# Zeroing the lists and the output from a small resident tile, spread over the steps of the attention, in a fused attention, MLP and top-2 MoE kernel

## The chip, the cores and the metric

One Trainium2 chip, of which the kernel uses a single core. Times are device microseconds of one execution. A core has a matrix engine (PE), whose weight loads show separately as PEld, a vector engine (DVE), an activation engine (ACT), a general engine (POOL) and a queue processor that does nothing but issue transfers (SP). Each runs its own list of instructions in order; they meet only through semaphores. Transfers that SP issues go through one hardware queue (q1) on the core's 16 DMA engines, transfers that POOL issues through a software queue (q0) on the same 16.

## The reference

```python
def _attn_ref(q, k, v, n_sink, window):           # 2 batches, 8 heads, 768 tokens, head size 64
    scores = scale * np.matmul(q, k.transpose(0, 1, 3, 2))
    keep = is_sink | in_window                    # 4 sink tokens, window of 128
    a = softmax(np.where(keep, scores, -1e9))
    return np.matmul(a, v)
def _moe_ref(x, w_in, w_out):                     # 1536 tokens, 512 -> 2048 -> 512
    h = x @ w_in
    return (h - np.tanh(h)) @ w_out
def _moe2_ref(x, w_gate, w_noise, noise, w1, w2): # 8 experts, 512 -> 1024 -> 512
    noisy_logits = x @ w_gate + np.log1p(np.exp(x @ w_noise)) * noise
    top2 = the two largest of each token; top2_w = softmax over these two
    out = np.zeros((N, D))
    for e, k: out[mask] += top2_w * (relu(x[mask] @ w1[e]) @ w2[e])
```

The three run one after the other on the same 1536 tokens.

## The kernel before

**Attention.** The tokens lie in 12 blocks of 128 (6 of each batch). A block has four pairs of heads, and a pair goes through PE (scores), DVE (L382: scale, mask and minimum), ACT (L395: exponential), POOL (L406: normalization), PE (L453: transposes) and PE again (L486: product with v). Each block needs its q, its k and its v, 256 KB each, loaded by SP (`att_load`, L260). Blocks 0 to 5 load k and v in place; from block 6 on a load lands in one of four `qr` buffers, ACT casts it (L289 q, L301 k, L314 v) and POOL takes the remainder (L290, L302, L315), which frees the buffer for a load some places later. In the listings `qr8_1` is the load of block 8's k (0 is q, 1 k, 2 v).

**First MLP.** From block 2 on its first layer (L606) and second layer (L638) run between the pairs. Its 96 steps `n` (a chunk of 256 tokens, a 128-wide piece of the hidden layer) are written out in order in the main loop; the first 24 run during the attention. Each piece of weights (`rawi`, `rawo`, 1 MB) is loaded by SP and split into two words by ACT and DVE (`split_d`, L202, with L215 on ACT and L216 on DVE as the first readers of a load). Two raw buffers of each kind are in turn, so a load waits for the split of the one two before it.

**Lists and output.** The router sends each token's row to two of 9 lists in device memory, `xs`, each a section of 1664 rows of 520 floats. The rows that an expert may read are zeroed ahead (`clear_rows`, L865): nine sections, for each one transfer of the rows in use (L871: 384, 512 or 256 rows, up to 1040 KB) and one of the last 8 floats of the rows that are left (L874: 36 to 44 KB in runs of 32 bytes). They read a zero tile that shares buffers (`x2T`) with the router. `route_setup` (L660) zeroes the whole output, 3 MB, by one transfer on POOL's queue (L675), and loads the router's small tables `wg_sb` (L661) and `noise_sb` (L662); DVE splits `wg_sb` into `wg_r` (L663, L664).

**Order.** The program is written in one sequence; a scheduler puts each engine's instructions in order from dependences and the written sequence, and may move an instruction far ahead of where it is written if it is ready. SP has eight semaphores in turn for its transfers: a transfer also waits for the one eight before it to have landed.

```python
        if n == 22:
            route_setup()
        if n == 56:
            clear_rows()
```

Of the kernel before, what the change touches and what calls it, by code (L numbers as in the profile page):

```python
# [9 lines left out]
F32 = mybir.dt.float32  # L10
# [6 lines left out]
P = 128  # L17
# [54 lines left out]
def kernel(ctx: ExitStack, tc: tile.TileContext, qkv, vsink, w64, wm, wgn, noise, out,  # L72
                                  n_sink, window):
    nc = tc.nc
    PSUM = bass.MemoryType.PSUM
    NBLK = qkv.shape[0]
    S = 768
    NB = S // P
    NT = NBLK * P
    E = 8  # L80
# [32 lines left out]
    cst = ctx.enter_context(tc.tile_pool(name="cst", bufs=1))  # L113
# [5 lines left out]
    PITCH = 520  # L119
# [472 lines left out]
    def a_at(n):  # L592
        g, c, u = seq[n]
        return g, c, u, 2 * g + u // 2

    def a_l1(n):
        g, c, u, d = a_at(n)
        w = wsp["i", d]
        s = u % 2
        h = bank("h", f"h{n}")  # L600
        hp[n] = h
        x, ts = x_cols(c * CT, (c + 1) * CT)
        t = 0
        for wa, xa in ((0, 0), (0, 1), (1, 0)):
            for k in range(4):
                nc.tensor.matmul(h[:, :CT], w[:, wa, k * 256 + s * P:k * 256 + (s + 1) * P],  # L606
                                 x[:, k, xa, ts], start=t == 0, stop=t == 11)
                t += 1

    def a_chain(n):  # L610

        h = hp.pop(n)
        th = gp.tile([P, CT], F32, tag="th", name=f"th{n}", bufs=2)
        nc.scalar.activation(th, h[:, :CT], AF.Tanh)  # L614
        yield
        nc.vector.tensor_sub(th, h[:, :CT], th)  # L616
        yield
        g = gp.tile([P, 2, CT], F32R, tag="g", name=f"g{n}", bufs=3)
        nc.scalar.copy(g[:, 0], th)  # L619
        yield  # L620
        nc.vector.tensor_sub(g[:, 1], th, g[:, 0].bitcast(F32))  # L621
        gt[n] = g
        yield

    def a_l2(n):
        gi, c, u, d = a_at(n)
        g = gt.pop(n)
        w = wsp["o", d]
        s = (u % 2) * 512
        end = c >= LATE  # L630
        first = u == 0 and not (end and gi == 3)
        done = u == 3 and not (end and gi == 2)
        if first:
            turn.reverse()
            acc[c] = [bank(turn[0] if gi else "a", f"acc{n}_{m}") for m in range(CB)]
        for m in range(CB):
            for t, (ga, wa) in enumerate(((0, 0), (1, 0), (0, 1))):
                i = nc.tensor.matmul(acc[c][m], g[:, ga, m * P:(m + 1) * P], w[:, wa, s:s + 512],  # L638
                                     start=first and t == 0, stop=done and t == 2)
        last_mm[0] = i  # L640
        if done:
            if gi == 0:
                x2s[c] = gp.tile([P, CB, PITCH], F32, tag="x2", name=f"x2_{c}", bufs=NC)
            for m in range(CB):
                x = x2s[c][:, m, :512]
                if gi == 0:
                    nc.scalar.copy(x, acc[c][m])
                else:
                    nc.vector.tensor_add(x, acc[c][m], x)
# [10 lines left out]
    def route_setup():  # L660
        nc.sync.dma_start(wg_sb, wgn)  # L661
        nc.sync.dma_start(noise_sb, noise)  # L662
        nc.vector.tensor_copy(wg_r[:, :, 0], wg_sb)  # L663
        nc.vector.tensor_sub(wg_r[:, :, 1], wg_sb, wg_r[:, :, 0].bitcast(F32))  # L664
        nc.gpsimd.memset(ones, 1.0)
        nc.gpsimd.memset(tri, 1.0)

        nc.gpsimd.affine_select(out=tri, in_=tri, compare_op=ALU.is_gt, fill=0.0, base=0,
                                pattern=[[1, P]], channel_multiplier=-1)
        nc.gpsimd.iota(idx, pattern=[[1, E]], base=0, channel_multiplier=0,  # L670
                       allow_small_or_imprecise_dtypes=True)
        nc.gpsimd.memset(macc, 0.0)
        zero = gp2.tile([P, 512], F32, tag="x2T", name="zero", bufs=2)
        nc.gpsimd.memset(zero, 0.0)
        nc.gpsimd.dma_start(out.rearrange("(t p) d -> p t d", p=P), zero[:, None, :].to_broadcast([P, NBLK, 512]))  # L675

    scat = []
    pend = []
# [179 lines left out]
    def width(v):  # L858
        return WA if v == 0 else WB if v == E else W
# [2 lines left out]
        w = width(v)  # L862
        return [(m, o, min(P, w - o)) for m, o in enumerate(range(0, w, P))]

    def clear_rows():  # L865

        zero = gp2.tile([P, 512], F32, tag="x2T", name="zrow", bufs=2)
        nc.gpsimd.memset(zero, 0.0)
        for v in range(E + 1):
            n = (width(v) + P - 1) // P  # L870
            nc.sync.dma_start(xs[v * SEC:v * SEC + n * P].rearrange("(p m) (b d) -> p (m b) d", p=P, b=2),  # L871
                              zero[:, None, :PITCH // 2].to_broadcast([P, 2 * n, PITCH // 2]))
            o = v * SEC + n * P
            nc.sync.dma_start(xs[o:(v + 1) * SEC, 512:].rearrange("(p m) d -> p m d", p=P),  # L874
                              zero[:, None, :8].to_broadcast([P, SEC // P - n, 8]))
        for c in range(NC):
            nc.gpsimd.memset(x2s[c][:, :, 518:], 0.0)
            for o in (0, 1):
                nc.gpsimd.iota(x2s[c].bitcast(I32)[:, :, 512 + o:513 + o], pattern=[[P, CB], [0, 1]],
                               base=c * CT + o * FAR, channel_multiplier=1)  # L880
# [251 lines left out]
    def mark():  # L1132
        return len(nc.cur_bb.bb.instructions)
# [22 lines left out]
    def emit(k, last):  # L1156

        while k > 0:
            if cur[0] is None:
                if not todo_split or todo_split[-1][1] > last:  # L1160
                    return
                cur[0] = todo_split.pop()
                cur.append(split_d(*cur[0]))
            try:
                next(cur[1])
                k -= 1
            except StopIteration:
                if cur[0][1] < 8 or cur[0][0] == "o" and cur[0][1] != EARLY_D:
                    load_next()
                cur[:] = [None]  # L1170

    def need(kind, d):
        while (kind, d) not in wsp:
            emit(1, d)
# [4 lines left out]
    def attend(k):  # L1179
        for _ in range(k):  # L1180
            next(slots, None)
            ns[0] += 1

    def attend_chunk(c):

        if not wide:
            attend(2 * (4 * CB * (c + 1) + LEND) - ns[0])
# [36 lines left out]
    def pull_routes():  # L1224
        if routes:
            with tc.high_priority():
                try:
                    next(routes[0])
                except StopIteration:
                    routes.pop(0)  # L1230

    gp2 = None
# [3 lines left out]
    for n in range(-3, N1):  # L1236
        marks["a", n] = mark()
        g, c, u, d = a_at(max(n, 0))
        ch = a_chain(n + 2) if 0 <= n + 2 < N1 else iter(())
        if n + 3 < N1:  # L1240
            g2, c2, u2, d2 = a_at(n + 3)
            if g2 == 0 and u2 == 0:
                attend_chunk(c2)
                if c2 == NC - 1:
                    if not wide:
                        att_ctx.__exit__(None, None, None)
                    gp2 = ctx.enter_context(tc.tile_pool(name="gp2", bufs=2))
                    ring[1] = gp2
            need("i", d2)
        last = min(2 * g + 3, 7) if gp2 else 1  # L1250
        m = g == 0 and n >= 0
        next(ch, None)
        if m:
            attend(1)
        next(ch, None)
        if n + 3 < N1:
            a_l1(n + 3)
        if m:
            attend(1)
        next(ch, None)  # L1260
        if n >= N1 - 7:
            emit((1, 1, 1, 1, 1, 1, 0)[n - N1 + 7], 11)
        elif g < 3 or n % 4 == 1:
            emit(1, last)
        if m:
            attend(1)
        next(ch, None)
        if n >= 0:
            need("o", d)
            a_l2(n)  # L1270
        if m:
            attend(1)
            emit(1, last)
        if n == 22:
            route_setup()
        if n == 56:
            clear_rows()
        if n >= 0 and g == NG1 - 1 and u == 3 and (c % 2 or c >= LATE):
            routes.append(route(c if c >= LATE else c - 1, c + 1))
            ends.append(c + 1)  # L1280
        if n < N1 - 1:
            for _ in range(3 if n <= PAIR else 2):
                pull_routes()
            issue(2 if PAIR <= n < PAIR + 4 else 1)
        if n == PAIR + 4:
            assert len(scat) == 2 * LATE * CB and not pend, (n, len(scat), len(pend))
            b_gather(0)
        if N1 - 3 <= n < N1 - 1:
            b_trans(0, (2 * (n - N1 + 3), 2 * (n - N1 + 3) + 1))
# [17 lines left out]
    for n in range(N1, N):  # L1307
        marks["a", n] = mark()
        e, u, d = b_at(n)
# [120 lines left out]
```

## Time and profile before

| | us |
|---|---|
| three runs, median (lowest to highest) | 774.65 (772.66 to 775.27) |
| profiled execution, its own time | 772.26 |
| span in its trace, first to last instruction | 770.0 |
| PE busy | 723.9 (94%) |
| DVE busy | 475.9 (62%) |
| ACT busy | 356.3 (46%) |
| POOL busy | 186.4 (24%) |
| granted PE clock, mean | 0.979 |

The rows come from one profiled execution, and lie on its clock, which begins with the span. The trace has each engine's instructions with the idle time ahead of them and what ended it. A row of SP is an issue: its duration is the time that SP was held, not the time of the transfer. [...]

### The profile page before, as it was taken

Reading aid. Unit: us, or ns where it says so; the run is one execution under the profiler, and the core shown is the slowest. Engines: PE = TensorE matmul, PEld = TensorE weight load, DVE = VectorE, ACT = ScalarE, POOL = GpSimd, SP = SyncE. Lnnn points to the kernel's source line nnn. Section 1 sums busy time; section 2 is a strip of 40 time slices with the busy share of each in tenths; the row PEclk is TensorE's granted clock in tenths of the full one; section 3 lists DMA queues with packets and bytes.
Section 4 is the critical chain, followed back from the end, with each engine's and each line's share of the span. In section 5 each row is a group of like instructions: output and inputs, shape, how many; then the busy total and the mean of one; then the engine's idle time right before and its main releaser. Section 6 shows DMA issues by size and latency. Waiting matters only on the chain.

```text
span 770.0 us, 12093 instructions
## 1 busy us (share of the span) xinstructions
PE 723.9 (94%) x4346; PEld 653.0 (85%) x4346; DVE 475.9 (62%) x1203; ACT 356.3 (46%) x785; POOL 186.4 (24%) x219
## 2 busy tenths in 40 slices
PE   6878999999699999999999979999999999999991
PEld 3565788888699999988888979999999999899991
DVE  5998678877587587446467766776646474544221
ACT  4977688776353344234346534444343434332110
POOL 4444355531000000000351231313131313132321
PEclk9999899999899999999999999999999999999996
DMA  7453111006998133000225388756757444444421
GB/s 263 138 178 109 56 51 61 2 1 206 297 287 233 56 110 110 1 1 1 84 112 167 125 237 237 213 164 194 193 186 192 164 155 160 143 139 165 143 84 35
DMA packets 62117, 104.96 MB, mean 136 GB/s; under 512 B 19629, under 2 KB 45869, under 8 KB 55392
## 3 DMA queue, kind: packets, MB, share of 16 engines
q1 hardware_dynamic: 54528, 80.20, 34.9%
q0 software_dynamic: 7376, 22.85, 8.7%
q10 hardware_dynamic: 144, 1.05, 0.3%
q8 instruction: 36, 0.59, 0.3%
q14 instruction: 33, 0.27, 0.1%
HBM read 79.12 MB, written 25.68 MB: 136 GB/s over the span
## 4 chain that ended last, share of the span: by engine, by line
PE 44%; issue 24%; DMA 15%; POOL 6%; DVE 6%; ACT 3%; POOLq 0%; SPq 0%; ACTq 0%; DVEq 0%
PE h L606 16%; PE acc L638 15%; DMA prev<-out,tab 6%; DMA out<-y,tab 5%; PE xb L486 4%; POOL out L1030 4%; PE s L371 3%; DMA rawo<-w 2%; POOL prev L883 2%; PE pt L453 2%; DVE e L382 1%; DMA rawi<-wm 1%; ACT e L395 1%; PE x2p L695 1%; PE y L1002 1%
## 5 line engine op out<-in xcount | busy, mean ns | idle before, releaser
L606 PE MATMUL h<-xT,wi 128*128 128x256 f32 x1152 | 160.9, 287 | 7.9 <-DVE th L616 5.9
L606 PEld LDWEIGHTS h<-xT,wi 128*128 128x128 f32 x1152 | 153.1, 192 | 14.9 <-DVE th L616 6.4
L978 PE MATMUL h<-xg,wi 128*128 128x424 f32 (+1 forms) x768 | 157.6, 354 | 4.0 <-ACT xg L961 3.9
L1002 PE MATMUL y<-hh,wo 128*128 128x424 f32 (+1 forms) x768 | 152.0, 347 | 0.7 <-DVE yt L1016 0.5
L638 PE MATMUL acc<-wo,g 128*128 128x512 f32 x576 | 151.1, 396 | 0.0
L978 PEld LDWEIGHTS h<-xg,wi 128*128 128x128 f32 x768 | 138.6, 190 | 8.7 <-ACT xg L961 5.0
L1002 PEld LDWEIGHTS y<-hh,wo 128*128 128x128 f32 x768 | 139.4, 188 | 4.1 <-DVE yt L1016 0.9
L638 PEld LDWEIGHTS acc<-wo,g 128*128 128x128 f32 x576 | 101.9, 189 | 16.5
L988 ACT ACTIVATE hh<-h 128x424 fp32r<-128x424 f32 (+1 forms) x64 | 32.6, 511 | 149.9 <-PE h L978 147.6
L1030 POOL DMA_INDIRECT out<-y,tab x33 | 41.4, 1255 | 189.7 <-DVE y L1029 189.4
L808 POOL DMA_INDIRECT xs<-x,sl x24 | 26.0, 1085 | 235.7 <-DVE th L616 183.7
L989 DVE SCALAR_TENSOR_TENSOR hh<-h,hh 128x424 fp32r<-128x424 f32 (+1 forms) x64 | 37.0, 578 | 73.9 <-ACT hh L988 69.8
L406 POOL TENSOR_TENSOR e<-e,nm 128x528 f32<-128x528 f32 (+1 forms) x48 | 50.1, 1044 | 81.3 <-DVE nm L404 45.5
L616 DVE TENSOR_TENSOR th<-h,th 128x256 f32<-128x256 f32 x96 | 40.4, 420 | 39.6 <-ACT th L614 37.1
L614 ACT ACTIVATE th<-h 128x256 f32<-128x256 f32 x96 | 36.6, 382 | 59.5 <-PE h L606 56.0
L619 ACT CAST g<-th 128x256 fp32r<-128x256 f32 x96 | 38.7, 404 | 55.0 <-PE acc L638 37.7
L395 ACT ACTIVATE e<-e,nm 128x264 f32<-128x264 f32 (+1 forms) x96 | 47.2, 492 | 22.5 <-DVE nm L382 20.3
L621 DVE TENSOR_TENSOR g<-th,g 128x256 fp32r<-128x256 f32 x96 | 43.2, 450 | 22.3 <-ACT g L619 21.4
L486 PE MATMUL xb<-pT,v 128*128 128x256 f32 x220 | 49.1, 352 | 3.6 <-DVE xT L501 2.2
L232 DVE TENSOR_TENSOR wi<-rawi,wi 128x1024 fp32r<-128x1024 f32 x32 | 39.1, 1223 | 21.6 <-ACT wi L231 21.5
L883 POOL DMA_INDIRECT prev<-out,tab x33 | 35.6, 1080 | 44.0 <-DMA out<-y,tab 34.6
L486 PEld LDWEIGHTS xb<-pT,v 128*128 128x128 f32 x220 | 33.7, 197 | 13.5 <-issue 5.3
(172 smaller groups left out, 888.8 us busy)
## 6 DMA issues: line engine op xcount, KB each, us to landing
rawi<-wm SPq DMA_DIRECT2D x31, 1024.0 KB
rawi<-w SPq DMA_DIRECT2D x8, 1024.0 KB
rawo<-w SPq DMA_DIRECT2D x8, 1024.0 KB
xs<-zrow SPq DMA_DIRECT2D x7, 1040.0 KB
xr<-xs SPq DMA_DIRECT2D x28, 224.0 KB
qr<-qkv SPq DMA_DIRECT2D x23, 256.0 KB
rawc<-wm SPq DMA_DIRECT2D x4, 1024.0 KB
out<-zero POOLq DMA_DIRECT2D x1, 3072.0 KB
```

What stands on the lines that cost most here:

```text
L232: nc.vector.tensor_sub(t[:, 1], r, t[:, 0].bitcast(F32))
L395: nc.scalar.activation(e[:, h], e[:, h], AF.Exp, bias=nm[:, h, 0:1], scale=-1.0, accum_out=nm[:, h, 2:3])
L406: nc.gpsimd.tensor_mul(e, e, nm[:, :, 3:4].to_broadcast([P, 2, C]))
L486: nc.tensor.matmul(o, l, r_, start=t == 0, stop=t == len(todo) - 1)
L606: nc.tensor.matmul(h[:, :CT], w[:, wa, k * 256 + s * P:k * 256 + (s + 1) * P], x[:, k, xa, ts], start=t == 0, stop=t == 11)
L616: nc.vector.tensor_sub(th, h[:, :CT], th)
L621: nc.vector.tensor_sub(g[:, 1], th, g[:, 0].bitcast(F32))
L638: i = nc.tensor.matmul(acc[c][m], g[:, ga, m * P:(m + 1) * P], w[:, wa, s:s + 512], start=first and t == 0, stop=done and t == 2)
L883: nc.gpsimd.indirect_dma_start(out=dst, out_offset=None, in_=src[:rows], in_offset=bass.IndirectOffsetOnAxis(ap=t[:n, m, c:c + 1], axis=0) ...
L978: nc.tensor.matmul(h[:, :width(e)], w[:, wa, k * 256 + s * P:k * 256 + (s + 1) * P], xg[e][:, k, xa, :width(e)], start=t == 0, stop=t == 11)
L1002: nc.tensor.matmul(yacc[e][m][:, :width(e)], w[:, wa, s + m * P:s + (m + 1) * P], g[:, ga], start=u == 0 and t == 0, stop=u == NU2 - 1 and ...
L1030: i = nc.gpsimd.indirect_dma_start(out=out[:, :], out_offset=bass.IndirectOffsetOnAxis(ap=t[:n, m, 1:2], axis=0), in_=y, in_offset=None, b ...
```

## The change

The zero tile becomes 128x260 and lives in the pool of constants. The nine sections go out one per step from step 2 of the first MLP on, and three transfers of 1 MB, now on SP's queue, zero the output in steps 11 to 13. What `clear_rows` did beside that (numbering the rows) stays at step 56, as `number_rows`.

```diff
@@ route_setup
-        zero = gp2.tile([P, 512], F32, tag="x2T", name="zero", bufs=2)
-        nc.gpsimd.memset(zero, 0.0)
-        nc.gpsimd.dma_start(out.rearrange("(t p) d -> p t d", p=P), zero[:, None, :].to_broadcast([P, NBLK, 512]))
@@
-    def clear_rows():
-
-        zero = gp2.tile([P, 512], F32, tag="x2T", name="zrow", bufs=2)
-        nc.gpsimd.memset(zero, 0.0)
-        for v in range(E + 1):
+    zero = cst.tile([P, PITCH // 2], F32, name="zero")
+
+    def clear(v):
+
+        if v == 0:
+            nc.gpsimd.memset(zero, 0.0)
+        if v <= E:
             n = (width(v) + P - 1) // P
             nc.sync.dma_start(xs[v * SEC:v * SEC + n * P].rearrange("(p m) (b d) -> p (m b) d", p=P, b=2),
-                              zero[:, None, :PITCH // 2].to_broadcast([P, 2 * n, PITCH // 2]))
+                              zero[:, None, :].to_broadcast([P, 2 * n, PITCH // 2]))
             o = v * SEC + n * P
             nc.sync.dma_start(xs[o:(v + 1) * SEC, 512:].rearrange("(p m) d -> p m d", p=P),
                               zero[:, None, :8].to_broadcast([P, SEC // P - n, 8]))
+        else:
+            o = (v - E - 1) * NT // 3
+            nc.sync.dma_start(out[o:o + NT // 3].rearrange("(p t) (b d) -> p (t b) d", p=P, b=2),
+                              zero[:, None, :2 * P].to_broadcast([P, NBLK // 3 * 2, 2 * P]))
+
+    def number_rows():
+
         for c in range(NC):
@@ main loop
+        if 2 <= n < E + 6:
+            clear(n - 2)
         if n == 56:
-            clear_rows()
+            number_rows()
```

The written order is not the order on the engines. On SP, at the weights of the first MLP after the attention, there stood in the kernel before (`rawo3` is the second-layer piece 3; `xs` transfers are the zeros):

```order
L277 DMA qr11_2_1871<-qkv 128x512
L179 DMA rawi3_2416<-w64 128x2048
L871 DMA xs_63<-zrow_3508 768x1x260
L874 DMA xs_63<-zrow_3508 1280x1x8
L871 DMA xs_63<-zrow_3508 1024x1x260
L179 DMA rawo3_2482<-w64 128x2048
L874 DMA xs_63<-zrow_3508 1152x1x8
L871 DMA xs_63<-zrow_3508 1024x1x260
```

and now, at the same place:

```order
L277 DMA qr11_2_1889<-qkv 128x512
L179 DMA rawi3_2439<-w64 128x2048
L179 DMA rawo3_2505<-w64 128x2048
L179 DMA rawi4_2575<-w64 128x2048
L179 DMA rawo4_2666<-w64 128x2048
```

The zeros are gone from between the weights. The sections stand earlier on SP, the first just behind the load of block 3's q, the others between the loads of blocks 3 to 9; the three pieces of the output come behind block 9's q, and the router's tables behind these. Before, SP had at that place only:

```order
L277 DMA qr8_1_1207<-qkv 128x512
L277 DMA qr8_2_1254<-qkv 128x512
L277 DMA qr9_0_1394<-qkv 128x512
L277 DMA qr9_1_1396<-qkv 128x512
L277 DMA qr9_2_1445<-qkv 128x512
```

and now:

```order
L870 DMA xs_63<-zero_96 1024x1x260
L277 DMA qr8_1_1213<-qkv 128x512
L277 DMA qr8_2_1260<-qkv 128x512
L873 DMA xs_63<-zero_96 1152x1x8
L870 DMA xs_63<-zero_96 512x1x260
L277 DMA qr9_0_1404<-qkv 128x512
L873 DMA xs_63<-zero_96 1408x1x8
L877 DMA out<-zero_96 1024x1x256 x3
L661 DMA wg_sb_89<-wgn 128x64
L662 DMA noise_sb_91<-noise 128x96
L277 DMA qr9_1_1406<-qkv 128x512
```

The table `wg_sb`, which SP issued right behind block 3's q, moved behind all the sections and the three pieces of the output, and `qr9_0`, ahead of it, waits as before for POOL's subtraction of block 8's k (L302) to free its buffer. On DVE the reader of that table moved too. Before, it stood in the attention of block 2 (`e_0_342`, `e_2_398`):

```order
L403 TENSOR_SCALAR nm_0_343<-nm_0_343 128x2
L663 CAST wg_r<-wg_sb 128x4x16
L382 ISA e_0_342,nm_1_371<-s_1_0_1_373,mask_146 128x264
L382 ISA nm_1_371 128x1
L404 RECIPROCAL nm_0_343<-nm_0_343 128x2
L228 SCALAR_TENSOR_TENSOR wi_245<-czi_247,wi_245 128x512
L664 TENSOR_TENSOR wg_r<-wg_sb,wg_r 128x4x16
```

and now, ahead of the first scores of block 8 (`e_0_1167`):

```order
L403 TENSOR_SCALAR nm_3_1122<-nm_3_1122 128x2
L404 RECIPROCAL nm_3_1122<-nm_3_1122 128x2
L501 TENSOR_TENSOR xT_72<-xb_2_1089,xT_72 64x2x128 x2
L663 CAST wg_r<-wg_sb 128x4x16
L664 TENSOR_TENSOR wg_r<-wg_sb,wg_r 128x4x16
L382 ISA e_0_1167,nm_0_1168<-s_0_0_0_1169,mask_130 128x264
L382 ISA nm_0_1168 128x1
L382 ISA e_0_1167,nm_0_1168<-s_0_0_1_1170,mask_130 128x264
L382 ISA nm_0_1168 128x1
L463 TENSOR_TENSOR pT_1_1153<-pt_1_0_1154,pT_1_1153 128x256
```

L663 waits for the load of `wg_sb` and for nothing else. On ACT and POOL the casts and subtractions of q and k of blocks 6 to 8 moved back by a few instructions: the cast of block 8's k (L301) stands now behind the exponentials of block 6's first pair, and its subtraction on POOL (L302) behind the normalization of that pair.

## Rows read from the trace of the kernel before

**Rows 1.** The page's busy times (us, share of the span and instructions).
```profile
PE 723.9 (94%) x4346; PEld 653.0 (85%) x4346; DVE 475.9 (62%) x1203; ACT 356.3 (46%) x785; POOL 186.4 (24%) x219
```

**Rows 2.** Waits of PE from 150 to 320 us: total, times, longest.
```profile
PE h L606 <- DVE th L616: 5.9, 1, 5.9
```

**Rows 3.** Timeline of DVE, 198 to 208 us: start, duration, instruction, idle time before.
```profile
198.58 0.42 DVE L621 TENSOR_TENSOR g<-th,g 128x256 fp32r<-128x256 f32 x1
205.88 0.69 DVE L216 TENSOR_SCALAR czo<-rawo 128x1024 int32<-128x1024 int32 x1 [6.87 <-DMA rawo<-w]
```

**Rows 4.** Timeline of SP's issues at the first sections, same columns.
```profile
178.98 0.33 SPq L179 DMA_DIRECT2D rawi<-w  x1
...
184.25 5.60 SPq L871 DMA_DIRECT2D xs<-zrow  x1
189.96 5.60 SPq L179 DMA_DIRECT2D rawo<-w  x1
```

**Rows 5.** Windows: length, busy of PE, PEld, DVE, ACT, POOL; PEclk, DMA share, GB/s.
```profile
6.00:12.00 6.00, 3.93 (x14) 2.64 (x14) 4.00 (x24) 3.54 (x16) 1.79 (x10) 1.00 1.02 388
96.00:102.00 6.00, 6.00 (x42) 5.20 (x41) 3.25 (x16) 4.31 (x15) 1.94 (x3) 1.00 0.00 0
198.00:206.00 8.00, 3.86 (x23) 3.10 (x21) 1.13 (x3) 0.14 (x1) 0.00 (x0) 0.91 1.07 282
206.00:214.00 8.00, 6.20 (x31) 5.82 (x32) 6.42 (x11) 5.07 (x9) 0.00 (x0) 0.66 1.08 289
214.00:222.00 8.00, 8.00 (x52) 7.24 (x51) 5.38 (x9) 4.88 (x10) 0.00 (x0) 1.00 1.07 291
```

**Rows 6.** Timeline of PE, 198 to 212 us.
```profile
197.73 1.32 PE L638 MATMUL acc<-wo,g 128*128 128x512 f32 x5
198.89 1.60 PE L606 MATMUL h<-xT,wi 128*128 128x256 f32 x12
...
207.80 2.93 PE L606 MATMUL h<-xT,wi 128*128 128x256 f32 x12 [5.94 <-DVE th L616]
210.53 1.74 PE L638 MATMUL acc<-wo,g 128*128 128x512 f32 x5
```

**Rows 7.** Issues of the zero tile: duration in ns (min/median/max), first and last start.
```profile
L871 SPq DMA_DIRECT2D xs<-zrow x9: 655/3507/5603, 182.9 to 238.7; - x9
L874 SPq DMA_DIRECT2D xs<-zrow x9: 540/630/3142, 183.6 to 239.9; - x9
```

**Rows 8.** Timeline of SP: issue of the load of block 8's k.
```profile
85.56 0.33 SPq L277 DMA_DIRECT2D qr<-qkv  x1
```

**Rows 9.** Timeline of ACT: cast of block 8's k, an exponential behind it.
```profile
88.61 0.61 ACT L301 CAST kT<-qr 128x512 fp32r<-128x512 f32 x1
...
92.49 0.39 ACT L395 ACTIVATE e<-e,nm 128x132 f32<-128x132 f32 x1
```

**Rows 10.** Chain of waits: start, duration of a 192 KB load, issue to landing.
```profile
2.18 2.91 DMA kF<-qkv
```

**Rows 11.** Timeline of DVE: the splitting of the router's table.
```profile
28.23 0.18 DVE L663 CAST wg_r<-wg_sb 128x64 fp32r<-128x64 f32 x1
...
29.35 1.08 DVE L664 TENSOR_TENSOR wg_r<-wg_sb,wg_r 128x64 fp32r<-128x64 f32 x1
```

**Rows 12.** Timeline of POOL: remainder of block 8's k, and a normalization.
```profile
89.92 1.29 POOL L302 TENSOR_TENSOR kT<-qr,kT 128x512 fp32r<-128x512 f32 x1
...
93.55 0.63 POOL L406 TENSOR_TENSOR e<-e,nm 128x264 f32<-128x264 f32 x1 [2.33 <-DVE nm L404]
```

**Rows 13.** Timeline of DVE at the first scores of block 8.
```profile
102.16 0.86 DVE L501 TENSOR_TENSOR xT<-xb,xT 64x256 fp32r<-64x256 f32 x2
103.34 0.43 DVE L382 CUSTOM_DVE_ANT_0 e<-s,mask 128x264 f32<-128x264 f32 x1 [0.32 <-PE s L371]
...
104.05 0.42 DVE L463 TENSOR_TENSOR pT<-pt,pT 128x256 fp32r<-128x256 f32 x1
```

**Rows 14.** Timeline of PE: the transposes of block 8's first pair.
```profile
105.03 0.38 PE L453 MATMUL pt<-ident,e 128*128 128x128 f32 x2
```

## Prediction

> **What bounds the kernel now.** I read the busy times first: PE is busy for 94% of the span [rows 1], so what PE loses is what the kernel loses, and a change that moves transfers can only show where PE waits for one. Then I read PE's waits in the stretch in which the zeros go out. Between 150 and 320 us there is one that counts, 5.9 us, for DVE's L616 [rows 2]. The timelines say why. DVE has nothing else to do from 199.0 on and stands at L216 until 205.88, when a load of `rawo` lands: 6.87 us idle [rows 3]. The instruction for which PE waits stands behind that one on DVE. SP had issued the load at 189.96, behind `rawi` and the first sections, and the issues themselves took 5.60 us [rows 4]: the queue was full, and the DMA engines show a share of 1.07 and 282 GB/s at that time [rows 5]. So the load came 15.9 us after its issue, and PE paid for 5.94 us of it [rows 6].
>
> It paid once more behind the stall. [...] That is 1.33 + 0.42 = 1.75 us.
>
> **What the change takes away.** The zeros no longer stand ahead of `rawo`, and the raw buffers are the same. `rawo` is then issued when its buffer is free, with one `rawi` ahead, and lands long before 199. The stall and its echo go: 5.94 + 1.75 = 7.7 us. Behind that, PE had no wait of a microsecond up to 320 us [rows 2], under a queue as full as this until 240 us [rows 5, 7], so nothing is next in line: I take all of the 7.7. POOL's memsets and its issue of the output's zeros lay where POOL waits anyway and count as nothing, as do the issues that SP no longer makes there, since SP is waited for only through what lands.
>
> **What it adds.** Nine sections, nine tails and the output's 3 MB are not new in size, but their place is. The sections fill SP's idle time from block 3 on. The price of each lies in what is queued behind it: a full section holds the queue for 3.51 us (the median issue while the queue was full) and its tail for 0.63 [rows 7], together 4.14. For most loads of blocks 3 to 7 that is covered, because the casts that read them moved back in the order of ACT as well. The tightest is block 8's k. Its load was issued at 85.56 and cast at 88.61 [rows 8, 9]; now the cast stands behind the exponential that ends at 92.49 + 0.39 = 92.88 [rows 9], so it has 7.3 us for a landing of 2.9 (a load of 192 KB from issue to landing [rows 10]; this one has 256) and one section of 4.14 ahead: 0.3 us to spare. I take zero for the sections. Bounds: below, DVE is rid of 1.26 us of table work in block 2 [rows 11], so -1.3; above, five loads (q and k of blocks 7 and 8, q of block 9) have a section or its tail ahead, and at the longest issue, 5.60 in place of 3.51 [rows 7], each would be 2.1 - 0.3 = 1.8 us late, with ACT standing in order: +9.
>
> The pieces of the output are another matter, because of what stands behind them. SP holds, in this order: `qr9_0`, a tail, three pieces of 1 MB, `wg_sb`. And DVE holds L663, which waits for `wg_sb`, in front of the scores of block 8. Step by step:
>
> 1. `qr9_0` needs the buffer that POOL's L302 of block 8 frees. That instruction ran at 89.92; it now follows the normalization that ends at 93.55 + 0.63 = 94.18 [rows 12], so it ends at 94.18 + 1.29 = 95.5, and SP issues then. The queue is empty at that time in the kernel before (share 0.00 from 96 to 102 [rows 5]), and holds no more than the half section that went ahead in the new one.
> 2. `qr9_0` lands 2.9 us later [rows 10], at 98.4. The tail takes 0.63, to 99.0. Three pieces of 1024 KB at the rate of the sections take 3 x 3.51 x 1024/1040 = 10.4, to 109.4. `wg_sb`, 32 KB, lands right behind them: 109.4.
> 3. DVE has finished L501, the instruction ahead, at 102.16 + 0.86 = 103.0 [rows 13]. It waits 6.4 us. Then come L663 and L664, 0.18 + 1.08 = 1.26 [rows 11], so the first L382 of block 8 starts at 110.7 in place of 103.34: 7.3 us late.
> 4. PE needs DVE's L463, which ended at 104.05 + 0.42 = 104.47, for its transposes at 105.03 [rows 13, 14]; they have 0.56 us to spare. PE is late by 6.7. The stall of the kernel before gives a second reading: 6.87 us of DVE cost 5.94 of PE [rows 3, 6], and in that proportion 7.3 costs 6.3. I take 6.7. PE is busy without a gap in the windows there [rows 5], so none of it is won back.
> 5. The clock falls as it did behind the other stall, for want of another row: 1.75.
>
> Together 8.4 us. Bounds: at the best rate in these rows, 388 GB/s [rows 5], the three pieces take 8.1, 2.3 less, and if the clock holds, 1.75 less: 4.4. At 5.60 us each they take 16.5, 6.1 more: 14.5.
>
> [...] The windows in which the sections ran, in runs of 1040 bytes, show 282 to 291 GB/s [rows 5], and the measurement decides.
>
> **The sum.** -7.7 + 8.4 = +0.7 us. Against the profiled execution's own 772.26 that is 773.0; the median of the three runs lies 2.4 us above that execution, and on it the forecast is 775.4. Its own range, from the bounds that are likely, is -2 to +4: 772.5 to 778.5. A measurement of this kernel can tell 0.3% from no change, 2.3 us, so the forecast reads as no change: one stall goes at 202 us, another comes at 105.
>
> **The rivals.**
>
> *Only the gain.* `wg_sb` lands before DVE comes to it, or PE has other work meanwhile. Then the change is worth -7.7, 767.0 us. For it: the order put the table's reader six blocks later than it was, together with the load, and the queue is idle from 96 to 102 us [rows 5]. Against it: 14 us of queue have to fit into the 7.5 between 95.5 and 103.0, and PE's next transposes need DVE within 2 us of that [rows 13, 14]. It decides if the pieces go out before `qr9_0`'s buffer is free, which the order on SP forbids, or at over twice the rate of the sections. A later load overtaking the zeros would do it too. [...] Chance 0.25, with the cases in which half of the wait is hidden.
>
> *The sections hurt too.* A section in front of a load makes ACT stand at a cast. The place is the q and k of blocks 7 to 9, and it decides where a load lands more than 0.3 us later than I reckon, for instance because 256 KB take longer than the 192 of the row or because the section was issued less than 4 us ahead. At 1.2 us for each of the five loads this is +6 on the forecast, 781.4. For it: the spare is 0.3 us in the one case that I can read exactly. Against it: an exponential pushed back there first uses up the other work that PE has in hand, and PE shows no gap in that stretch [rows 5]. Chance 0.27.
>
> *The stall at 202 stays.* The change doesn't do what it says: `rawo` is late for another reason, such as its buffer, and the new wait comes on top: +8.4, 783.1. But SP issued `rawo` at 189.96, the moment it was through with the section at 184.25 + 5.60 = 189.85 [rows 4], so no buffer held it, and this is the least likely. Chance 0.06.
>
> **How the numbers follow.** The forecast has 0.42. Same, within 0.3% of 774.65 (772.3 to 777.0): 0.30 of the forecast's 0.42, and 0.06 from the halfway cases of the first two rivals: 0.36. Faster: 0.21 from the first rival and 0.05 from the forecast's lower end: 0.26. Slower: the rest of the forecast (0.07), of the second rival (0.25) and of the third (0.06): 0.38. The range goes from the centre of the first rival to just over that of the second, 767 to 782; outside lie half of the first (0.1) and the upper part of the other two (0.1).
>
> **What would show it.** Right: DVE idle for about 6 us ahead of L663 near 103, released by the load of `wg_sb`; PE idle for some 6.7 ahead of an L453, with a granted clock under 1.00 in that window; no wait of PE for L616 around 200; transfers at a share of 1 from 97 to 109 and near nothing from 182 to 190 but weights. Wrong: DVE at L663 without idle time; `rawo` again as the releaser of L216; idle time of ACT ahead of L289 or L301, released by `qr`, in blocks 7 to 9. The sum is wrong above all if PE's loss at 105 is not within 2 us of 6.7, or if the clock does not fall behind it.

## The result, and the profile after

The changed kernel takes 765.01 us in the median of four runs (762.02 to 767.55), against 774.89 us for the kernel before: a ratio of 0.989, with a 95% interval of 0.985 to 0.993. The forecast was 775.4 in a range of 767 to 782, so the time lies 2 us under the range. Both mechanisms of the forecast are in the profile; their sum is not.

The profiled execution took 767.55 us, 4.7 us less than that of the kernel before. PE is as full as it was [rows 1]:

```profile
PE 722.1 (94%) x4346; PEld 652.2 (85%) x4346; DVE 473.8 (62%) x1203; ACT 356.2 (47%) x785; POOL 185.5 (24%) x217
```

**The stall at 202 us is gone.** The waits of PE from 110 to 400 us name no L606 any more [rows 2]; the only entry is

```profile
PE xb L486 <- ACT st L435: 1.0, 3, 0.4
```

SP issues `rawo` at 192.77 in 0.33 us instead of standing in the issues for 5.60 [rows 4], and DVE comes to its L216 without idle time [rows 3]. SP, then DVE:

```profile
192.77 0.33 SPq L179 DMA_DIRECT2D rawo<-w  x1
```
```profile
203.00 0.69 DVE L216 TENSOR_SCALAR czo<-rawo 128x1024 int32<-128x1024 int32 x1
```

**The wait for the router's table is there.** DVE's timeline around L663 [rows 11, 13]:

```profile
99.70 0.86 DVE L501 TENSOR_TENSOR xT<-xb,xT 64x256 fp32r<-64x256 f32 x2
104.74 0.19 DVE L663 CAST wg_r<-wg_sb 128x64 fp32r<-128x64 f32 x1 [4.18 <-DMA wg_sb<-wgn]
104.97 0.23 DVE L664 TENSOR_TENSOR wg_r<-wg_sb,wg_r 128x64 fp32r<-128x64 f32 x1
105.22 0.43 DVE L382 CUSTOM_DVE_ANT_0 e<-s,mask 128x264 f32<-128x264 f32 x1
```

DVE is idle for 4.18 us, released by the load of `wg_sb`. PE stands behind it at the transposes of [rows 14] (they and the scores ahead of them are those of block 7, counted from 0 as the loads are, not of block 8 as I called them; their times stand); six second-layer products take 2.76 us just behind that, where 1.55 is usual:

```profile
101.13 1.58 PE L606 MATMUL h<-xT,wi 128*128 128x256 f32 x12
106.50 0.66 PE L453 MATMUL pt<-ident,e 128*128 128x128 f32 x2 [3.79 <-DVE pT L463]
...
108.85 2.76 PE L638 MATMUL acc<-wo,g 128*128 128x512 f32 x6
```

The windows show both places (columns as in [rows 5]; PEclk is the clock granted to PE as a share of full speed, DMA share the time of the packets under way over that of the core's 16 DMA engines, so over 1 where more than 16 are under way): the granted clock falls to 0.83 and 0.60 behind the new wait, and is 1.00 with PE full where the old one was.

```profile
96.00:102.00 6.00, 6.00 (x44) 5.03 (x44) 2.68 (x11) 4.95 (x14) 3.88 (x7) 1.00 1.09 385
102.00:108.00 6.00, 2.21 (x14) 1.51 (x13) 2.56 (x11) 2.21 (x7) 0.79 (x2) 0.83 0.53 189
108.00:114.00 6.00, 6.00 (x28) 4.75 (x27) 4.08 (x16) 3.05 (x10) 2.76 (x3) 0.60 0.14 44
...
198.00:206.00 8.00, 8.00 (x53) 7.22 (x52) 7.21 (x12) 4.29 (x10) 0.00 (x0) 1.00 0.39 132
206.00:214.00 8.00, 8.00 (x53) 7.27 (x53) 7.14 (x11) 5.62 (x11) 0.00 (x0) 1.00 0.54 178
```

What stands ahead of `wg_sb` on SP is what the forecast said: `qr9_0`, a tail, the three pieces of the output, then the table. `qr9_0` goes out when POOL's L302 has ended. The times differ. POOL, then SP:

```profile
90.65 1.30 POOL L302 TENSOR_TENSOR kT<-qr,kT 128x512 fp32r<-128x512 f32 x1
```
```profile
91.97 0.33 SPq L277 DMA_DIRECT2D qr<-qkv  x1
92.35 0.54 SPq L873 DMA_DIRECT2D xs<-zero  x1
92.93 3.70 SPq L877 DMA_DIRECT2D out<-zero  x3
96.69 3.12 SPq L661 DMA_DIRECT2D wg_sb<-wgn  x1
```

**A clock by instruction.** The rest of the text compares traces by the starts of the same instruction: a row of the scores (L382, 20.4 us in the first trace of the kernel before) and products of L606 (130.4, 190.4, 223.7 us there, and the last one of the first MLP). From their starts, in each trace, come these stretches in us; the columns bear these times without their fractions, and 222 stands for the product at 223.7. The last column runs from that last product to the end of the span.

| trace | start to 20 | 20 to 130 | 130 to 190 | 190 to 222 | 222 to the last L606 | to the end |
|---|---|---|---|---|---|---|
| before | 20.4 | 110.0 | 60.0 | 33.3 | 196.2 | 350.1 |
| after | 20.6 | 114.0 | 59.9 | 25.4 | 194.9 | 350.5 |

Read from left to right: +0.2, +4.0, -0.1, -7.9, -1.3, +0.4, together -4.7. The +4.0 is made of two parts: up to 100 us the changed kernel draws ahead (L501, the instruction ahead of the wait, begins at 99.70 in place of 102.16, 2.5 us earlier), and from 112 us on every score and product is 4.2 us later than before the change. So the wait costs 6.7 us at its place, 3.79 of idle PE and 2.9 of products that run slow behind it.

### The profile page after: what moved, and what is told of

Read it like the earlier page. It is cut to its first block, busy times and chain, and to the rows that moved or that the text cites. A ratio compares the mean times of both kernels' runs of the same rounds, so it can differ in the third digit from the quotient of the medians.

```text
span 765.2 us, 12079 instructions
## 1 busy us (share of the span) xinstructions
PE 722.1 (94%) x4346; PEld 652.2 (85%) x4346; DVE 473.8 (62%) x1203; ACT 356.2 (47%) x785; POOL 185.5 (24%) x217
## 5 line engine op out<-in xcount | busy, mean ns | idle before, releaser
L606 PE MATMUL h<-xT,wi 128*128 128x256 f32 x1152 | 157.6, 283 | 1.2 <-DVE th L616 1.2
L606 PEld LDWEIGHTS h<-xT,wi 128*128 128x128 f32 x1152 | 150.4, 189 | 8.2 <-DVE th L616 1.6
L486 PEld LDWEIGHTS xb<-pT,v 128*128 128x128 f32 x220 | 33.3, 196 | 15.6 <-issue 6.2
## 6 DMA issues: line engine op xcount, KB each, us to landing
xr<-xs SPq DMA_DIRECT2D x28, 224.0 KB, 6.4
```

Of the source, the lines that this page charges most:

```text
L486: nc.tensor.matmul(o, l, r_, start=t == 0, stop=t == len(todo) - 1)
```

## The experiments

Ratios are to the kernel before, on the same chip and with a 95% interval. The table of stretches at the end of this section gives the place of each difference.

**The changed kernel again.**

> The changed kernel once more. Theory A (the stall at 202 us is gone, 7.9 us; the wait for wg_sb at 103 us takes back some 6.7 with its slow clock; the attention ahead of it is 2.5 us earlier because a slow-clock stretch of the kernel before, 75 to 81 us, is shorter): ratio to before 0.985 to 0.994, L663 idle for 3.5 to 4.5 us, PE 5 to 7 us later between 100 and 112 us than at 100. Theory B (the wait at 103 hardly counts, and the gain comes from the attention): ratio the same, but no loss between 100 and 112 us.

766.4 us, ratio 0.991 (0.988 to 0.995). DVE waits 4.56 us, and the loss from 100 to 112 us is 7.1 us (the same instruction is 5.4 us ahead of the first trace of the kernel before at 100 us, and 1.7 us behind it at 112); both lie just over what theory A had. Theory B is out.

```profile
102.14 0.19 DVE L663 CAST wg_r<-wg_sb 128x64 fp32r<-128x64 f32 x1 [4.56 <-DMA wg_sb<-wgn]
```

**The tables first.** `route_setup` moves from step 22 to step 1, and SP issues `wg_sb` at 11.8 us, ahead of the first section.

```diff
-        if n == 22:
+        if n == 1:
             route_setup()
```

> The changed kernel with route_setup at step 1 of the first MLP, so that the loads of wg_sb and noise_sb go out ahead of the first section. Theory A: L663 has no wait, the idle time of PE at 103 us and the slow clock behind it go, 5 to 7 us faster than the changed kernel (about 759, ratio to before 0.980). Theory B, the wait hardly counts: 0 to 1 us faster. Rival C: the loads of block 9's k and v, behind the three pieces of the output, take the wait's place: ACT idle ahead of L301 at 105 to 110 us, 764 to 766.

763.27 us, ratio 0.988 (0.984 to 0.991), 3.1 us under the changed kernel in the same job. L663 stands in block 2 again, DVE does not wait for it, and PE no longer waits 3.8 us at L453. Its waits from 60 to 420 us begin with:

```profile
PE xb L486 <- DVE xT L501: 4.5, 3, 1.8
PE xb L486 <- ACT st L435: 1.0, 3, 0.4
```

So the wait is real and worth taking away, but for 3 us rather than the 5 to 7 expected. From 20 to 130 us the kernel takes 109.6 us (108.7 with a further edit, below) against 114.0 and 112.9, 3.3 to 5.3 less, where the place itself showed 6.7 and 7.1. Rival C is not seen: from 20 to 130 us ACT waits for a load once, 0.2 us at an L289.

**The sections alone, first try.** The output is zeroed on POOL's queue again, written at step 22.

```diff
+        nc.gpsimd.dma_start(out.rearrange("(p t) (b d) -> p (t b) d", p=P, b=2),
+                            zero[:, None, :2 * P].to_broadcast([P, NBLK * 2, 2 * P]))
...
-        if 2 <= n < E + 6:
+        if 2 <= n < E + 3:
             clear(n - 2)
```

> The sections alone are moved; the output is zeroed by one transfer on POOL's queue at step 22 as before (from the same zero tile, in runs of 1 KB). Theory A: wg_sb stands behind the last section only, no wait of over 2 us for it, and rawo lands in time at 202 because 3 MB less than 9 are on the queue: 758 to 761. Rival D: the output's 3 MB alone hold rawo up: idle time of DVE at L216 near 200 us, 3 us or more, 763 or more.

773.77 us, ratio 1.001 (0.998 to 1.004): neither theory. The zero tile is ready at 6.4 us, so the scheduler put the 3 MB there and not at step 22. POOL's timeline, and the waits of PE in the first 30 us:

```profile
6.74 1.61 POOL L663 DMA_DIRECT2D out<-zero  x1 [0.18 <-POOL ones L667]
```
```profile
PE s L371 <- DVE nm L382: 8.1, 4, 6.1
PE s L371 <- DMA kF<-qkv: 4.2, 2, 3.3
```

The loads of the first blocks share the engines with it (in the first 20 us 4.13 MB moved on SP's queue and 1.85 MB on POOL's, at 299 GB/s together), and the scores of 20.4 us come at 28.1. The run says nothing of the sections, but what 3 MB cost where PE waits for loads. The stall near 202 is gone in it too.

**The output alone.** The sections stay where they were before the change.

```diff
-        nc.gpsimd.dma_start(out.rearrange("(t p) d -> p t d", p=P), zero[:, None, :].to_broadcast([P, NBLK, 512]))
...
+        if 11 <= n < 14:
+            clear_out(n - 11)
         if n == 56:
             clear_rows()
```

> The output alone is moved: three pieces on SP's queue from block 3 on, the sections where they were before the change. Theory A: the 3 MB were 8 of the 15.9 us that rawo took, so it lands some 8 us earlier, near 198, the wait of 5.9 us at 202 goes or falls under 1 us, and later weights may be late by less than 1 us: 766 to 768. Rival E: the sections ahead of rawo (and the full ring that holds SP 5.6 us an issue) are what delays it: the wait stays at 4 us or more, 771 to 775.

760.71 us, ratio 0.985 (0.981 to 0.988): 5.7 us under the changed kernel in the same job. Only the same kernel with the late table work (760.75, below) is as fast. `rawo` goes out between two sections in 0.33 us, and PE has no wait at L606:

```profile
179.83 1.78 SPq L878 DMA_DIRECT2D xs<-zrow  x1
184.82 0.33 SPq L179 DMA_DIRECT2D rawo<-w  x1
...
191.04 0.33 SPq L179 DMA_DIRECT2D rawi<-w  x1
```

That `rawo` lands 6.1 us after its issue, and the three loads of weights behind it after 8.5 to 11.0, beside the sections; all that waits for one of them is ACT, for 0.4 us. The DMA engines are as full from 190 to 222 us as in the kernel before, but PE has no idle time. Before, and then here (columns as in [rows 5]):

```profile
190.00:222.00 32.00, 26.06 (x157) 23.46 (x156) 19.34 (x31) 15.92 (x28) 0.00 (x0) 0.89 1.06 300
```
```profile
190.00:222.00 32.00, 32.00 (x208) 29.10 (x207) 25.33 (x40) 17.61 (x35) 0.00 (x0) 1.00 1.11 271
```

Rival E falls: the sections alone did not hold `rawo` for as long as DVE could do without it. With the output's pieces among the loads of blocks 3 to 5 (`wg_sb` behind them is issued at 35.2 us) there is no wait at 103 us either. The gain was larger than the 766 to 768 expected, since the whole stall went, with its slow clock: 8 to 9 us from 190 to 222, where I had counted 6 to 8. The medians in this job lie 11.3 us apart (771.97 less 760.71); the other 2 to 3 us are in no single stretch.

**The kernel before again**, for a second and a third profile.

> The kernel before once more, for a second profile: the changed kernels are 2.5 to 3.6 us ahead of it at 100 us, and this tells how much of that is scatter of the attention. Theory F (the start of the attention scatters by some us from execution to execution, and the lead is no more than that): first scores of block 8 at 100 to 102 us in place of 103.34, the slow-clock stretches at other places. Theory G (the lead belongs to the change): within 0.7 us of 103.34. By both the wait of 5.9 us near 202 us is there, within 1 us.

> The kernel before, for a third profile. Theory F (scatter): first scores of block 8 anywhere from 98 to 104 us; 33 to 35 us from the product at 190 us to the one at 222; 344 to 352 us from the first product of the experts to the end.

774.4 and 768.63 us in the profiled executions. The stall is in both, as the first entry of PE's waits from 150 to 320 us, the one and then the other:

```profile
PE h L606 <- DVE th L616: 6.9, 1, 6.9
```
```profile
PE h L606 <- DVE th L616: 6.7, 1, 6.7
```

The scores of [rows 13] come 4.6 us earlier in the first of them than in the trace the forecast was made from (98.8 us, where theory F had 100 to 102) and 3.9 in the second, so the lead of 2.5 to 5.4 us that the changed kernel showed at 100 us is no more than scatter. Theory G, within 0.7 us, does not hold here. Part of it lies at the start (18.6 us to the first row of the table below, not 20.4), part in the stretch from 72 to 84 us, where the granted clock was 0.74 and 0.69 in the first trace and 1.00 in this one.

**The table work out of block 2.** Only the kernel before, with L663 behind a product of step 21.

```diff
-        nc.vector.tensor_copy(wg_r[:, :, 0], wg_sb)
+        i = nc.vector.tensor_copy(wg_r[:, :, 0], wg_sb)
+        wait_for(i, last_mm[0])
```

> The kernel before with one edit: L663, the first reader of wg_sb on DVE, also waits for a product of step 21 of the first MLP, so that the 1.26 us of table work leave block 2 for 200 us; all transfers stand where they stood. Theory G (DVE, over 90% busy from 20 to 70 us, sets the pace there, and the lead comes from the table work that left it): 1.3 to 3 us earlier at 100 us, ratio 0.996 to 0.999. Theory F: no lead beyond 0.5 us that holds, ratio 1.000 within its interval. The stall near 202 stays.

774.9 us, ratio 0.9965 (0.993 to 0.9995). That ratio is one that theory G had, and its interval just excludes 1; but the profile shows no lead at all, 110.2 us from 20 to 130. The same edit in the two better kernels (in the first of them the two loads alone stand at step 1, the rest of `route_setup` at step 22 again):

> The changed kernel with the loads of wg_sb and noise_sb ahead of the first section, and L663 behind a product of step 21: neither the wait at 103 us nor the table work in block 2. Theory A with G: 1.5 to 3 us faster than the kernel with the early loads alone, which was at 0.9876 of the kernel before: 0.984 to 0.986. Theory F: the same as that kernel, 0.987 to 0.989.

764.28 us, 0.984 (0.980 to 0.987).

> The kernel with the output's three pieces moved and the sections left at step 56 (0.9847 of the kernel before), and L663 behind a product of step 21. Theory G: the table work stands in block 3 there, where DVE is as full: 0 to 1.3 us faster, 0.983 to 0.985. Theory F: no difference, 0.984 to 0.986. Both: no wait for wg_sb, no wait of over 1 us near 202 us.

760.75 us, 0.980 (0.977 to 0.984). The medians lie within 1.0 us of the kernels without the edit (763.27, 760.71), measured in an earlier job on another chip; the lower ratios come from a median of the kernel before of 776.78 in this job against 771.97 in that one. All three ratios with the edit are about 0.4% under those without it, some 3 us, but all three rest on that one sample of the kernel before, and the traces show no steady gain from 20 to 130 us. So neither theory is shown: what the table work costs in block 2 is between nothing and some 3 us.

**The sections alone, second try.** As in the first, with POOL's transfer behind a product of step 21.

```diff
-        nc.gpsimd.dma_start(out.rearrange("(p t) (b d) -> p (t b) d", p=P, b=2),
+        i = nc.gpsimd.dma_start(out.rearrange("(p t) (b d) -> p (t b) d", p=P, b=2),
                             zero[:, None, :2 * P].to_broadcast([P, NBLK * 2, 2 * P]))
+        wait_for(i, last_mm[0])
```

> The sections alone moved, as in the changed kernel, and the output zeroed in one transfer on POOL's queue that waits for a product of step 21, so that it starts near 180 us as in the kernel before. Theory A (the stall near 202 needs both kinds of zeros at once on the 16 engines; each alone leaves rawo in time; and without the output's pieces wg_sb lands some 8 us earlier): no wait of over 1 us at L606 near 200, 25 to 26 us from the product at 190 us to the one at 222 us of the kernel before, wait at L663 under 1 us, ratio to before 0.984 to 0.990. Rival D (the output's 3 MB alone hold rawo): wait of 3 us or more near 200, ratio 0.990 to 0.996.

762.52 us, ratio 0.986 (0.983 to 0.990). There is no wait at L606, and 25.4 us from 190 to 222, as theory A had it. But the test missed its place: POOL issued the 3 MB at 197.99 us, some 15 us later than meant (182.8 in the kernel before), when the `rawo` of the stall, issued at 184.59, had landed. POOL's issue, and the issues of 184.59, 203.40 and 197.99 to landing:

```profile
197.99 1.63 POOL L663 DMA_DIRECT2D out<-zero  x1 [29.07 <-PE acc L638]
```
```profile
rawo<-w SPq DMA_DIRECT2D x1, 1024.0 KB, 4.8
rawi<-w SPq DMA_DIRECT2D x1, 1024.0 KB, 10.2
out<-zero POOLq DMA_DIRECT2D x1, 3072.0 KB, 15.0
```

The load that met the 3 MB, `rawi` at 203.40, took 10.2 us to land in place of 4.8, and its first reader came only at 224.0. So rival D was not put to the test where the stall is. An estimate: in the changed kernel 10.2 us lie between the issue of `rawo` (192.77) and its reader (203.00), so by these 10.2 us the 3 MB alone would have cost a few tenths of a us there and not 3. L663 waits longer than expected, 2.89 us at 93, but at another place, between two pairs of block 6. DVE, then PE:

```profile
93.24 0.20 DVE L666 CAST wg_r<-wg_sb 128x64 fp32r<-128x64 f32 x1 [2.89 <-DMA wg_sb<-wgn]
```
```profile
94.42 0.77 PE L371 MATMUL s<-kT,qT 64*128 64x132 f32 x6 [1.06 <-DVE nm L382]
```

PE loses 1.06 of the 2.89, for it had products of the first MLP in hand.

**The runs of the sections.** The same bytes in runs of 1024 B.

```diff
-            nc.sync.dma_start(xs[v * SEC:v * SEC + n * P].rearrange("(p m) (b d) -> p (m b) d", p=P, b=2),
-                              zero[:, None, :].to_broadcast([P, 2 * n, PITCH // 2]))
+            p = 78 if n == 3 else 104
+            nc.sync.dma_start(xs[v * SEC:v * SEC + n * P].rearrange("r c -> (r c)").rearrange("(p m d) -> p m d", p=p, d=256),
+                              zero[:p, None, :256].to_broadcast([p, n * P * PITCH // (p * 256), 256]))
```

> The changed kernel with the same bytes of the sections written in runs of 1024 B (from 104 or 78 partitions) in place of 1040. Theory H (16 bytes over 1 KB make a packet take 53 ns in place of 46): packets of the sections at 46 to 47 ns, 350 to 390 GB/s while a section goes out in place of 260 to 290; by it the attention and wg_sb's landing gain 0 to 2 us, ratio to the kernel before 0.986 to 0.991. Rival I (the sections are slow because of where they write or of loads beside them): 53 ns and 260 to 290 GB/s as before, ratio 0.989 to 0.992.

765.17 us, ratio 0.988 (0.985 to 0.991), no different from the changed kernel. The packet records decide for H on the packets: a median of 46 ns for 1024 B (51 to 54 for 1040 B in the other traces). The rate over a whole stretch did not rise: five windows from 30 to 92 us have 167 to 248 GB/s, against 197 to 276 in the second profile of the changed kernel, so that number of the expectation was not met. But the run changed something else as well: its sections come from 104 or 78 partitions in place of 128, and by the packet records about 13 of their packets were under way at a time, where the changed kernel shows 16 to 18. So it does not tell what the shorter runs alone would do for the rate. The time shows nothing of them: the scheduler put L663 behind block 7's last pair here, DVE waits there just as long, and PE 4.4 us behind it.

```profile
112.19 0.20 DVE L663 CAST wg_r<-wg_sb 128x64 fp32r<-128x64 f32 x1 [4.17 <-DMA wg_sb<-wgn]
```

**The output alone again**, one profile.

> The kernel with the output alone moved, for a second profile. Theory F: 79 to 83 us from the scores at 20 us to those at 103 (79.0 in its first profile, 80.2 to 83.2 in those of the kernel before). Theory J (its order of the attention is truly faster): 78.5 to 79.5. Both: 25.4 us from the product at 190 us to the one at 222.

763.74 us; 80.5 us from the scores at 20 us to those at 103, and 107.4 from 20 to 130, where the first profile had 106.0 and that with the late table work 105.7. Theory J in its narrow form is out.

| trace | start to 20 | 20 to 130 | 190 to 222 | 222 to the last L606 | to the end |
|---|---|---|---|---|---|
| before, three | 18.6 to 20.4 | 107.2 to 110.0 | 33.3 to 34.7 | 195.5 to 197.2 | 350.1 to 354.8 |
| before, late table work | 20.8 | 110.2 | 33.4 | 196.5 | 357.5 |
| changed, twice | 19.1, 20.6 | 112.9, 114.0 | 25.4 | 194.9 | 350.5, 352.6 |
| tables first, twice | 20.6 | 108.7, 109.6 | 25.4 | 194.9, 195.2 | 352.6, 354.3 |
| sections alone, first try | 28.1 | 114.0 | 25.4 | 194.9 | 352.1 |
| sections alone, second try | 18.5 | 107.8 | 25.4 | 194.9 | 353.6 |
| runs of 1024 B | 18.5 | 112.6 | 25.4 | 194.9 | 352.1 |
| output alone, three | 18.5 to 20.6 | 105.7 to 107.4 | 25.4 | 194.9 to 195.3 | 350.5 to 355.6 |

For the stretch from 20 to 130 us the windows tell idle time from slow clock. The first trace of the kernel before, its third, the changed kernel and the output alone:

```profile
20.36:130.36 110.00, 99.55 (x597) 76.94 (x598) 89.17 (x317) 85.89 (x249) 51.09 (x51) 0.95 0.32 101
```
```profile
19.06:126.48 107.42, 96.89 (x598) 74.76 (x598) 89.28 (x317) 85.47 (x247) 51.26 (x51) 0.98 0.32 104
```
```profile
20.57:134.54 113.97, 100.01 (x597) 76.95 (x598) 87.06 (x317) 85.86 (x249) 50.95 (x51) 0.96 0.72 199
```
```profile
20.57:126.58 106.01, 95.91 (x598) 74.30 (x599) 89.12 (x317) 85.17 (x249) 51.36 (x51) 0.98 0.40 126
```

The length less PE's busy time is its idle time: 10.5, 10.5, 14.0 and 10.1 us. The two traces of the kernel before differ by their clock and not by idle time; the changed kernel has 3.5 us more idle time, about the 3.79 of its new wait, at a clock as low as that of the first.

## Why the prediction was wrong, step by step

**The gain, -7.7: right in place and size, its reading too narrow.** From 190 to 222 us the changed kernels take 25.4 us and the kernel before 33.3, 34.7 and 34.1, so the stall with its slow clock costs 7.9, 9.4 and 8.7; the trace that I had was the mildest of three. I put it down to the sections ahead of `rawo` and counted POOL's transfer of the output as nothing. That is not so: the stall goes when the output alone is moved and the sections stay. So the sections by themselves do not make it; POOL's transfer beside them, on the same engines at once, does. That POOL's transfer by itself would not make it either is an estimate (the second try); no run has the 3 MB alone at that place. The landings agree: 1 MB of weights landed 4.8 us after its issue by itself, 6.1 to 11.0 beside the sections, 10.2 beside the 3 MB and 15.9 beside both.

**The loss, +8.4: the mechanism right, the sizes off.** Step 1 had `qr9_0` issued at 95.5; it was 91.97, because the same normalization and L302 ran 3.5 us earlier in this execution. Step 2 had 13.9 us from there to `wg_sb`'s landing; it was 12.8 (104.74 - 91.97), and inside it the three pieces moved at 385 GB/s (window 96 to 102), 8.2 us for 3.1 MB, not the 10.4 that I took from the rows of the sections. The 10.4 was no price of a transfer alone: the rows it came from had weights beside the sections. The bound of 8.1 was the better value. In step 3, DVE came to L663 at 100.56 instead of 103.0, 2.5 us earlier as well. The wait was 4.18 instead of 6.4, and L664 took 0.23 instead of 1.08. Step 4 gave PE 6.7 us idle; it was 3.79. Step 5 took 1.75 for the clock, from 2.93 less 1.60 and 1.74 less 1.32 in [rows 6], in a stretch for which that trace shows a granted clock of 0.50 (205 to 211 us); here it was 2.9 (6.7 less 3.8), at 0.50 from 106 to 112 us. At the place that is 6.7 us, and 7.1 in the second profile, in place of 8.4. Over the whole stretch from 20 to 130 us it is 3.3 to 6.2 us against the tables first and the second try of the sections, and 2.9 to 6.8 against the kernel before; timed, taking the wait away was worth 3.1.

**"I take zero for the sections": borne out where it was bounded.** In the changed kernel ACT waits for a load once between 20 and 110 us, for block 8's k, the one load whose 0.3 us of spare were worked out:

```profile
89.89 0.62 ACT L301 CAST kT<-qr 128x512 fp32r<-128x512 f32 x1 [0.40 <-DMA qr<-qkv]
```

So the rival "the sections hurt too" is out. "Only the gain" gave 767.0, the number nearest to the result, but for a wrong reason: `wg_sb` does come too late. It landed 8.0 us after its issue and did not overtake the zeros: its last packet ended at 104.03 us, the last of the three pieces at 103.91. "The stall at 202 stays" is out.

**What was missing from the sum.** Between 222 us and the last product of the first MLP the changed kernels are 0.6 to 2.4 us shorter (194.9 against 195.5 to 197.2). Part of it lies at 404 us in the first trace, where PE waited 0.57 us at L695 for DVE; the rest is spread and was not followed up.

**The step that failed** is the term +8.4, which measured 6.7 and 7.1 at its place: mis-sized by its start (step 1), its rate (step 2) and the wait that came of them (4.18 for 6.4, and 3.79 of PE for 6.7). With it failed the sum of two large terms of opposite sign that I forecast as no change. With the measured terms it reads -7.9 to -9.4, +3.3 to +7.1, -0.6 to -2.4: -1.4 to -8.4. That term is not the whole of the miss. Between the first two traces I was off by 5.4 us (+0.7 against -4.7): 1.7 are this term, 0.2 the gain, 1.3 the stretch behind 222 us, and the largest part, 2.5, is the lead at 100 us, no more than scatter; the small stretches go the other way. So the other fault is the base. Executions of the kernel before ran from 766 to 781 us, the medians of its four jobs from 772 to 777, and its single traces differ by 3 us from 20 to 130 us and by 5 behind the last L606. I carried -2 to +4 us for the likeliest case, about what the base alone scatters by.

**Open.** The timed ratios, 0.989 and 0.991, are 7 to 8 us (the medians themselves lie 9.9 and 5.6 apart); the stretches of the first two traces explain about 5. I can't say where the rest lies, beyond that it is no more than the scatter of single traces; the table work that left block 2, up to some 3 us by its ratios, may be part of it. Nor did I settle why the kernels with the output alone moved are up to 4 us quicker from 20 to 130 us than the tables first and the second try of the sections. PE idles 9.2 to 10.4 us there in the former and 11.3 to 12.6 in the latter, and ACT waits for a load for 1.3 us at most.

## What to carry to other kernels

Zeros that depend on nothing are sent as early as the scheduler finds room, not at the step at which they are written (here three pieces together at 93 us, and once 3 MB at 6.7 us, for 8 us at the start). Give such a transfer a dependence or write it behind the small loads: 32 KB behind 3 MB stopped DVE for 4.2 us and PE for 3.8, and behind that stop the granted clock was 0.50 from 106 to 112 us, which cost another 2.9 us. Before moving everything, move one half. The 3 MB of the output alone brought the whole gain (760.7 us); moving the other 9 MB as well put the table behind all of them and brought the new wait.

## What the runs showed of the hardware

The packets of 1040 B took 51 to 54 ns in the median, those of 1024 B 46, from the packet records. The fastest tenth of the 1040-B packets took up to 47, so part of the difference can come from the loads beside them. With nothing else on the queue the 1024-B packets of the output moved 385 GB/s (window 96 to 102 of the changed kernel), and the windows in which sections and weights were under way together 282 to 291 [rows 5]. The packets of the tails, 32 B each, took 9 ns in the median, so by an estimate 36 KB of them cost about what 225 KB cost in runs of 1024 B (1152 packets of 9 ns against 225 of 46).
